# Attention with two exp engines: quarter-row pieces of the shifted exp tiles on GpSimd, placed beside VectorE's PSUM reads

## The chip, the cores and the metric

The kernel runs on one core of a Trainium2 chip. The metric is the device time of one execution in microseconds. I quote medians of a kernel's runs; a ratio is the mean time of one kernel's fast runs over the mean of the other's fast runs of the same rounds, so it is not quite the ratio of the medians. Among the fast runs the granted TensorE clock lay between 0.98 and 1.00, and the runs of one kernel spread by up to 0.8%, mostly with the lower clock at the slower end.

TensorE does matrix products into PSUM, ScalarE (ACT) does exp, VectorE (DVE) and GpSimd (POOL) do elementwise work; GpSimd does not read PSUM here. "Page" below is the printed summary of a profile.

## The reference, cut to what matters

```python
x = A_x                                   # 1 x 2048 x 512, bf16
xn = _layernorm(x)
q = heads(xn @ wq)                        # 32 heads of 16
k, v = xn @ wk, xn @ wv                   # one head of keys and values for all
p = softmax(q @ k.T * 16 ** -0.5)         # 32 x 2048 x 2048
s = merge(p @ v) @ wo
g = silu(silu(xn @ w1) @ w2)              # two-layer side branch
return x + s * g
```

The work is the 134 million exps. In tiles of 128 keys x 512 queries they are 2048 *score tiles*. Each is one matmul of the scores, one exp, and value matmuls.

## The kernel before

A planner in Python simulates the five engines with fixed durations and emits one static order for each, with semaphores. A score tile has two ways through:

- **ScalarE**: one exp over two or three PSUM banks at once, then one value matmul per tile.
- **VectorE**: a linear map of the score to the bits of a bf16 number, which is a coarse exp with a periodic error. Four copies of it with shifted bits, weighted in the value matmuls, average the error away. One tile costs one *eviction* (PSUM to SBUF, 128x512) and a quarter of four *shifts* (SBUF to SBUF, 128x2048, one for four tiles), and five value matmuls.

The eviction and the shift (everything else cut):

```python
# eviction, one per tile
bt.P[i] = pl.add(Task(DV, T_P, lambda v, b=b, i=i, bb=bt.b: v.tensor_scalar(
    db_sb[:, bb, i * NQ:(i + 1) * NQ], bank(b), 128.0 * LOG2E, 128.0 * SHIFT_BETA + 16256.0,
    op0=ALU.mult, op1=ALU.add), [("ps", b)], [("Db", bt.b, i)], ...))
# shift, four per batch of four tiles
pl.add(Task(DV, T_SH, lambda v, s=s, j=j, bb=bt.b: v.tensor_scalar(
    ds_sb[:, s, :], db_sb[:, bb, :], SHIFT[j], None, op0=ALU.add), ...))
```

How many tiles go to VectorE is decided while planning:

```python
def want_d(banks_left=True):
    # ... cut
    if dve_backlog() > DVE_LIMIT:        # 4000 ns
        return False
    return True
# in do_S, for each score phase of TensorE:
want = 2 if bl < TWO_LIMIT else 1        # 1500 ns of VectorE backlog
nd = min(cap, 4 - len(banks), len(need), want)
if nd < min(want, len(need)) and len(banks) == 3 and bl < LEND_LIMIT:
    nd, lend = nd + 1, True              # take a bank from ScalarE's three
```

The softmax here doesn't subtract the row's maximum and nothing guards it: scores larger than these inputs give would overflow.

## Time and profile before

770.08 us when first timed (768.81 to 770.92, 3 runs).

| from 100 to 730 us | TensorE | VectorE | ScalarE | GpSimd |
|---|---|---|---|---|
| busy, us of 630 | 590.4 | 617.3 | 630.0 | 0.0 |
| share | 94% | 98% | 100% | 0% |

The page: busy time of each engine, the chain of work that ended last, and three groups of instructions. A group's columns are line, engine, operation, tiles, forms and count, then busy us and mean ns of one, then the engine's idle us just before them.

```profile
span 768.8 us, 19950 instructions
PE 708.2 (92%) x8669; PEld 201.6 (26%) x8669; DVE 738.2 (96%) x1290; ACT 748.2 (97%) x773; POOL 20.0 (3%) x46
...
ACT 95%; DVE 1%; PE 1%; DMA 1%; issue 0%; SPq 0%; DVEq 0%
...
L1206 ACT ACTIVATE pa_sb<-ps 128x1024 bf16<-128x1024 f32 (+1 forms) x694 | 737.2, 1391 | 2.8 <-PE ps L697 2.7
L873 DVE TENSOR_SCALAR db_sb<-ps 128x512 uint16<-128x512 f32 x492 | 327.0, 685 | 11.2 <-PE ps L697 9.4
L907 DVE TENSOR_SCALAR ds_sb<-db_sb 128x2048 uint16<-128x2048 uint16 x492 | 321.7, 684 | 0.9
```

ScalarE's exp (L1206) waits 2.8 us in all, and the chain is ScalarE for 95%: the time is the amount of ScalarE's work. Evictions (L873) and shifts (L907) number 492 each, so 24% of the tiles go to VectorE, and VectorE is full. Three engines are full or nearly so, and one is empty.

Bars are longer than the distance between starts, because the start of one instruction overlaps the end of the last. The timeline of VectorE (start us, length us, merged runs of equal instructions) shows the distance:

```profile
312.30 0.68 DVE L907 TENSOR_SCALAR ds_sb<-db_sb 128x2048 uint16<-128x2048 uint16 x1
312.90 0.68 DVE L873 TENSOR_SCALAR db_sb<-ps 128x512 uint16<-128x512 f32 x1
313.50 0.68 DVE L907 TENSOR_SCALAR ds_sb<-db_sb 128x2048 uint16<-128x2048 uint16 x1
314.10 0.68 DVE L550 SCALAR_TENSOR_TENSOR tmp_sb<-t_sb,ps 128x512 bf16<-128x512 bf16 x1
```

Each costs 0.60 us of VectorE, not 0.68. A tile therefore takes 1.20 us of VectorE, half of it the shifts, and a quarter of a shift is 0.15 us.

### The profile page before, as it was taken

Reading aid. Unit: us, or ns where it says so; the run is one execution under the profiler, and the core shown is the slowest. Engines: PE = TensorE matmul, PEld = TensorE weight load, DVE = VectorE, ACT = ScalarE, POOL = GpSimd, SP = SyncE. Lnnn points to the kernel's source line nnn. Section 1 sums busy time; section 2 is a strip of 40 time slices with the busy share of each in tenths; the row PEclk is TensorE's granted clock in tenths of the full one; section 3 lists DMA queues with packets and bytes.
Section 4 is the critical chain, followed back from the end, with each engine's and each line's share of the span. In section 5 each row is a group of like instructions: output and inputs, shape, how many; then the busy total and the mean of one; then the engine's idle time right before and its main releaser. Section 6 shows DMA issues by size and latency. Waiting matters only on the chain.

```text
span 768.8 us, 19950 instructions
## 1 busy us (share of the span) xinstructions
PE 708.2 (92%) x8669; PEld 201.6 (26%) x8669; DVE 738.2 (96%) x1290; ACT 748.2 (97%) x773; POOL 20.0 (3%) x46
## 2 busy tenths in 40 slices
PE   8999999999989999999989999999998999999985
PEld 3322222222222222222222222222222222222222
DVE  7699999999999999999999999999999999999996
ACT  4999999999999999999999999999999999999995
POOL 5400000000000000000000000000000000000000
PEclk9999999999999999999999999999999999999999
DMA  9300000000000000000000010000000000000000
GB/s 312 88 1 2 2 2 1 2 2 2 2 1 15 29 15 2 1 2 2 2 1 2 15 29 15 2 2 2 3 1 2 15 15 29 2 2 2 1 2 28
DMA packets 11429, 12.57 MB, mean 16 GB/s; under 512 B 1808, under 2 KB 10768, under 8 KB 11344
## 3 DMA queue, kind: packets, MB, share of 16 engines
q1 hardware_dynamic: 10288, 11.28, 4.6%
q8 instruction: 69, 1.13, 0.6%
q10 hardware_dynamic: 1056, 0.03, 0.1%
q14 instruction: 16, 0.13, 0.1%
HBM read 8.95 MB, written 2.10 MB: 14 GB/s over the span
## 4 chain that ended last, share of the span: by engine, by line
ACT 95%; DVE 1%; PE 1%; DMA 1%; issue 0%; SPq 0%; DVEq 0%
ACT pa_sb L1206 91%; ACT t_sb L525 4%; ACT t_sb L548 1%; DMA ds_sb<-in_A_x_dram 1%; DVE stats_sb L359 1%; PE ps L697 0%; PE ps L440 0%; SPq L317 0%; PE ps L398 0%; PE ps L968 0%; PE ps L414 0%; DVE xnT_sb L425 0%; DVE f_sb L985 0%; DVE ob_sb L565 0%; DVE on_sb L996 0%
## 5 line engine op out<-in xcount | busy, mean ns | idle before, releaser
L1206 ACT ACTIVATE pa_sb<-ps 128x1024 bf16<-128x1024 f32 (+1 forms) x694 | 737.2, 1391 | 2.8 <-PE ps L697 2.7
L873 DVE TENSOR_SCALAR db_sb<-ps 128x512 uint16<-128x512 f32 x492 | 327.0, 685 | 11.2 <-PE ps L697 9.4
L907 DVE TENSOR_SCALAR ds_sb<-db_sb 128x2048 uint16<-128x2048 uint16 x492 | 321.7, 684 | 0.9
L697 PE MATMUL ps<-qt_sb,kt_sb 32*128 32x512 bf16 x2048 | 272.9, 384 | 47.7 <-ACT pa_sb L1206 35.9
L968 PE MATMUL ps<-ds_sb,v_sb 128*32 128x512 bf16 x1968 | 260.0, 383 | 0.8 <-DVE ds_sb L907 0.5
L968 PE MATMUL ps<-pa_sb,v_sb 128*32 128x512 bf16 x1556 | 257.5, 385 | 0.8 <-ACT pa_sb L1206 0.4
L697 PEld LDWEIGHTS ps<-qt_sb,kt_sb 32*128 32x128 bf16 x2048 | 69.9, 91 | 337.7 <-ACT pa_sb L1206 273.4
L968 PE MATMUL ps<-db_sb,v_sb 128*32 128x512 bf16 x492 | 133.7, 384 | 2.6 <-DVE f_sb L985 1.9
L968 PEld LDWEIGHTS ps<-ds_sb,v_sb 128*32 128x32 bf16 x1968 | 65.4, 95 | 56.5 <-issue 28.1
L968 PEld LDWEIGHTS ps<-pa_sb,v_sb 128*32 128x32 bf16 x1556 | 63.6, 94 | 52.5 <-issue 34.1
L398 PE MATMUL ps<-xnT_sb,w_sb 128*32 128x512 bf16 x896 | 76.6, 385 | 0.6 <-DVE u_sb L527 0.4
L398 PE MATMUL ps<-w_sb,u_sb 128*32 128x512 bf16 x896 | 75.8, 385 | 0.0
L525 ACT ACTIVATE t_sb<-ps 128x512 bf16<-128x512 f32 x56 | 48.8, 872 | 0.0
L527 DVE SCALAR_TENSOR_TENSOR u_sb<-t_sb,ps 128x512 bf16<-128x512 bf16 x56 | 38.1, 680 | 0.6 <-ACT t_sb L525 0.3
L968 PEld LDWEIGHTS ps<-db_sb,v_sb 128*32 128x32 bf16 x492 | 33.0, 94 | 20.4 <-issue 10.4
L398 PEld LDWEIGHTS ps<-xnT_sb,w_sb 128*32 128x32 bf16 x896 | 19.5, 94 | 33.1 <-issue 24.0
L985 DVE STREAM_TRANSPOSE f_sb<-ps 128x512 f32<-128x512 f32 x32 | 22.7, 710 | 5.0 <-PE ps L968 4.9
L398 PEld LDWEIGHTS ps<-w_sb,u_sb 128*32 128x32 bf16 x896 | 18.6, 94 | 31.0 <-issue 26.0
L398 PE MATMUL ps<-xnT_sb,wq_sb 128*32 128x512 bf16 x256 | 20.5, 383 | 0.0
L398 PE MATMUL ps<-wo_sb,on_sb 128*32 128x512 bf16 x256 | 19.9, 383 | 0.6 <-DVE on_sb L996 0.6
L548 ACT ACTIVATE t_sb<-ps 128x512 bf16<-128x512 f32 x16 | 13.8, 860 | 0.0
L989 DVE TENSOR_TENSOR otr_sb<-f_sb,rcp_sb 128x256 bf16<-128x256 f32 x32 | 13.3, 416 | 0.0
(46 smaller groups left out, 160.3 us busy)
## 6 DMA issues: line engine op xcount, KB each, us to landing
w_sb<-in_B_w_dram SPq DMA_DIRECT2D x2, 1792.0 KB, 13.2
xr_sb<-in_A_x_dram SPq DMA_DIRECT2D x16, 128.0 KB, 2.4
out_dram<-ob_sb SPq DMA_DIRECT2D x16, 128.0 KB, 1.7
ds_sb<-in_A_x_dram SPq DMA_DIRECT2D x3, 512.0 KB, 7.9
ds_sb<-in_A_x_dram SPq DMA_DIRECT2D x4, 128.0 KB, 2.6
wq_sb<-in_A_wq_dram SPq DMA_DIRECT2D x1, 512.0 KB, 5.9
wo_sb<-in_A_wo_dram SPq DMA_DIRECT2D x1, 512.0 KB, 14.5
kt_sb<-kt_sb SPq DMA_DIRECT2D x4, 64.0 KB, 2.3
```

The source lines that it names most:

```text
L359: ts_ = pl.add(Task(DV, 593.0, lambda v, t=t: v.bn_stats(stats_sb[:, t, :], x_tile(t)), [xkey(t)], [("st", t)], 1 + j, gate=(lambda: q_don ...
L398: last = h.matmul(bank(b)[32 * j:32 * (j + 1), 0:n], lhsT=lhs(j), rhs=rhs, start=start, stop=stop, tile_position=(0, 32 * j), skip_group_c ...
L525: t1 = Task(AC, 477.0, lambda a: a.activation(t_sb[:, k, :], bank(b), ACT.Tanh, scale=0.5), [("ps", b)], [("t", k)], 0)
L527: t2 = Task(DV, T_P, lambda v: v.scalar_tensor_tensor(out=u_sb[:, ft, :], in0=t_sb[:, k, :], scalar=1.0, in1=bank(b), op0=ALU.add, op1=ALU ...
L548: t1 = Task(AC, 477.0, lambda a: a.activation(t_sb[:, k, :], bank(b), ACT.Tanh, scale=0.25), [("ps", b)], [("t", k)], 0)
L697: return pe.matmul(bank(b), lhsT=kt_sb[32 * i:32 * i + 32, g % 2, kt * P:(kt + 1) * P], rhs=qt_sb[32 * i:32 * i + 32, (g // 2) % NQR, :], ...
L873: bt.P[i] = pl.add(Task(DV, T_P, lambda v, b=b, i=i, bb=bt.b: v.tensor_scalar(db_sb[:, bb, i * NQ:(i + 1) * NQ], bank(b), 128.0 * LOG2E, 1 ...
L907: pl.add(Task(DV, T_SH, lambda v, s=s, j=j, bb=bt.b: v.tensor_scalar(ds_sb[:, s, :], db_sb[:, bb, :], SHIFT[j], None, op0=ALU.add), [("Db" ...
L968: h = pe.matmul(bank(OB)[32 * i:32 * (i + 1), :], lhsT=lhs, rhs=rhs, start=s0, stop=s1, tile_position=(0, 32 * i), skip_group_check=True)
L985: t1 = pl.add(Task(DV, T_TR, lambda v: v.transpose(f_sb[:, k, :], bank(OB)), [("ps", OB)], [("F", k)], 1, [norm.get(("m", g - 2))]))
L989: t3 = pl.add(Task(DV, 332.0, lambda v: v.tensor_tensor(o3[:, :, val:val + DH], f3[:, :, val:val + DH], rcp_sb[:, k, :].unsqueeze(2).to_br ...
L1206: op = pl.place(AC, 0.8333 * NQ * n + T_AF, lambda a: a.activation(pa_sb[:, s, 0:n * NQ], ps[:, b0 * 512:(b0 + n) * 512], ACT.Exp), [("ps" ...
```

## The change

Intent: give part of the shifts to idle GpSimd. The Trainium skill, "SBUF — State Buffer", section "Who interferes with whom", says that VectorE shares one pair of SBUF ports with GpSimd, that a VectorE tensor_scalar from SBUF to SBUF can run in a mode that takes this pair for the whole instruction, that the second comer "fully blocks", and that an instruction with at most one SBUF input outside those modes does not contend. So a shift on GpSimd is cut in quarters of 128x512, each about as long as one eviction; a quarter is planned only while VectorE's last planned instruction is a PSUM read (or another one-port instruction) with at least half a piece left to run; and the planner holds back either engine's two-port instruction while the other's runs. Each shift is offered to both engines, and whichever takes it first removes it from the other.

```diff
+T_PC, PC_FIT = 600.0, 0.5
@@ Planner
+    def locked(self, eng, ports):
+        if ports != 2 or eng not in self.lock:
+            return 0.0
+        return self.lock[PO if eng == DV else DV]
@@ place
-            t0 = max(self.clk[eng], self.ready(eng, reads, writes))
+            t0 = max(self.clk[eng], self.ready(eng, reads, writes), self.locked(eng, ports))
+        if eng in self.lock and ports == 2:
+            self.lock[eng] = op.end
@@ make_shifts: split(bt, s, j) replaces the single VectorE task
+            sh.whole = pl.add(Task(DV, T_SH, ..., on_place=placed_dv, ports=2))
+            for i in range(4):
+                tk = Task(PO, T_PC, lambda g, i=i: g.tensor_scalar(
+                    ds_sb[:, s, i * NQ:(i + 1) * NQ], db_sb[:, bt.b, i * NQ:(i + 1) * NQ], 1.0, SHIFT[j],
+                    op0=ALU.mult, op1=ALU.add), ...
+                    gate=lambda i=i: (sh.owner is None if i == 0 else sh.owner == PO and sh.chunks[i - 1].op is not None)
+                    and beside_psum_read(), ports=2)
+                tk.after = before_po
+                sh.chunks.append(pl.add(tk))
+        def beside_psum_read():
+            last = pl.order[DV][-1]
+            return last.ports == 1 and last.end - max(pl.clk[PO], pl.lock[DV], pl.lock[PO]) >= PC_FIT * T_PC
# cut: ports=2 on three other VectorE tasks, bookkeeping, tuple priorities, the case of an empty order, and
# before_po, which makes a piece wait for the last VectorE instruction planned to be done when it starts
```

More of the change, by code (lines that the diff above doesn't have):

```diff
@@ L47, with __init__ @@
 class Op:
-    __slots__ = ("eng", "emit", "deps", "idx", "inc", "val", "t0", "end", "vis", "dma", "know", "sem", "waits")
+    __slots__ = ("eng", "emit", "deps", "ports", "idx", "inc", "val", "t0", "end", "vis", "dma", "know", "sem", "waits")
 class Task:
-    __slots__ = ("eng", "dur", "emit", "reads", "writes", "prio", "preds", "op", "on_place", "dma", "gate")
-    def __init__(self, eng, dur, emit, reads=(), writes=(), prio=5, preds=(), on_place=None, dma=0, gate=None):
+    __slots__ = ("eng", "dur", "emit", "reads", "writes", "prio", "preds", "op", "on_place", "dma", "gate", "ports", "after")
+    def __init__(self, eng, dur, emit, reads=(), writes=(), prio=5, preds=(), on_place=None, dma=0, gate=None, ports=1):
+        self.ports, self.after = ports, None
         self.eng, self.dur, self.emit = eng, dur, emit
@@ L79, in __init__ @@
         self.dma_t = 0.0
+        self.lock = {DV: 0.0, PO: 0.0}
     def vis(self, op, eng):
@@ L107, in ready, with place @@
         return r
-    def place(self, eng, dur, emit, reads, writes, dma=0, t0=None):
+    def place(self, eng, dur, emit, reads, writes, dma=0, t0=None, ports=1, after=None):
         op = Op()
-        op.eng, op.emit, op.inc, op.val, op.know, op.sem = eng, emit, False, 0, None, None
+        op.eng, op.emit, op.inc, op.val, op.know, op.sem, op.ports = eng, emit, False, 0, None, None, ports
         deps = self.deps(eng, reads, writes)
+        if after is not None:
+            deps.append(after)
         seen = set()
@@ L147, in avail @@
             return None
-        return self.ready(task.eng, task.reads, task.writes)
+        return max(self.ready(task.eng, task.reads, task.writes), self.locked(task.eng, task.ports))
     def place_task(self, task):
         self.tasks[task.eng].remove(task)
-        task.op = self.place(task.eng, task.dur, task.emit, task.reads, task.writes, task.dma)
+        task.op = self.place(task.eng, task.dur, task.emit, task.reads, task.writes, task.dma,
+                             ports=task.ports, after=task.after() if task.after else None)
         if task.on_place:
@@ L162, in best @@
             if r <= t + 25.0:
-                key = (task.prio() if callable(task.prio) else task.prio, k)
+                p = task.prio() if callable(task.prio) else task.prio
+                key = (p if isinstance(p, tuple) else (p,), k)
                 if now is None or key < now[0]:
@@ L377, in bass_recurrent_scan__grouped_kv_mqa__dense_activation_silu__prompt_kernel @@
                     op0=ALU.subtract, op1=ALU.mult),
-                    [xkey(t), ("rs", pr), ("mv", t)], [("xn", t % 4)], 1 + t // 4, [t2],
+                    [xkey(t), ("rs", pr), ("mv", t)], [("xn", t % 4)], 1 + t // 4, [t2], ports=2,
                     gate=lambda t=t: t < 4 or t - 4 in t_done))
@@ L565, in final @@
             t2 = Task(DV, 333.0, lambda v: v.tensor_tensor(ob_sb[:, tt % 4, :], fin_sb[:, k, :], xr_sb[:, tt % 4, :], ALU.add),
-                      [("fin", k), ("xr", tt % 4)], [("ob", tt % 4)], 1, [t1, xr_task[tt], out_task.get(tt - 4)])
+                      [("fin", k), ("xr", tt % 4)], [("ob", tt % 4)], 1, [t1, xr_task[tt], out_task.get(tt - 4)], ports=2)
             t3 = Task(SP, 60.0, lambda e: e.dma_start(of.rearrange("(t p) d -> p t d", p=P)[:, tt, :], ob_sb[:, tt % 4, :]),
@@ L899, in make_shifts @@
                     j = bt.nsh
-                    def placed(pop, j=j, s=s, bt=bt):
-                        release(bt)
-                        for i in range(4):
-                            kt = bt.slots[i]
-                            pvq[bt.g][i].append((pop, v_lhs(j + 1, bt.g, kt), ds_sb[:, s, i * NQ:(i + 1) * NQ].bitcast(BF16),
-                                                 ds_keys(s) + v_reads(j + 1, kt), ("s", s)))
-                    pl.add(Task(DV, T_SH, lambda v, s=s, j=j, bb=bt.b: v.tensor_scalar(
-                        ds_sb[:, s, :], db_sb[:, bb, :], SHIFT[j], None, op0=ALU.add),
-                        [("Db", bt.b, i) for i in range(4)], ds_keys(s),
-                                lambda g=bt.g: URGENT if g == st["gO"] and nleft[g] <= CLOSING else 6, list(bt.P.values()), on_place=placed))
+                    split(bt, s, j)
@@ new lines, in bass_recurrent_scan__grouped_kv_mqa__dense_activation_silu__prompt_kernel, with split, queue, placed_dv @@
+        class Shift:
+            pass
+        shifts = []
+        def split(bt, s, j):
+            sh = Shift()
+            sh.owner = None
+            def queue(pop, i):
+                kt = bt.slots[i]
+                pvq[bt.g][i].append((pop, v_lhs(j + 1, bt.g, kt), ds_sb[:, s, i * NQ:(i + 1) * NQ].bitcast(BF16),
+                                     [("Ds", s, i)] + v_reads(j + 1, kt), ("s", s)))
+            def placed_dv(pop):
+                sh.owner = DV
+                for tk in sh.chunks:
+                    pl.tasks[PO].remove(tk)
+                release(bt)
+                for i in range(4):
+                    queue(pop, i)
+            def placed_po(pop, i):
+                if sh.owner is None:
+                    sh.owner = PO
+                    pl.tasks[DV].remove(sh.whole)
+                queue(pop, i)
+                if i == 3:
+                    release(bt)
+            sh.whole = pl.add(Task(DV, T_SH, lambda v: v.tensor_scalar(
+                ds_sb[:, s, :], db_sb[:, bt.b, :], SHIFT[j], None, op0=ALU.add),
+                [("Db", bt.b, i) for i in range(4)], ds_keys(s),
+                lambda: URGENT if bt.g == st["gO"] and nleft[bt.g] <= CLOSING else 6,
+                list(bt.P.values()), on_place=placed_dv, ports=2))
+            sh.chunks = []
+            for i in range(4):
+                tk = Task(PO, T_PC, lambda g, i=i: g.tensor_scalar(
+                    ds_sb[:, s, i * NQ:(i + 1) * NQ], db_sb[:, bt.b, i * NQ:(i + 1) * NQ], 1.0, SHIFT[j],
+                    op0=ALU.mult, op1=ALU.add),
+                    [("Db", bt.b, i)], [("Ds", s, i)], (0 if i else 1, -len(shifts), i), list(bt.P.values()),
+                    on_place=lambda pop, i=i: placed_po(pop, i),
+                    gate=lambda i=i: (sh.owner is None if i == 0 else sh.owner == PO and sh.chunks[i - 1].op is not None)
+                    and beside_psum_read(), ports=2)
+                tk.after = before_po
+                sh.chunks.append(pl.add(tk))
+            shifts.append(sh)
@@ L912, in bass_recurrent_scan__grouped_kv_mqa__dense_activation_silu__prompt_kernel, with before_po @@
+        def beside_psum_read():
+            if not pl.order[DV]:
+                return False
+            last = pl.order[DV][-1]
+            return last.ports == 1 and last.end - max(pl.clk[PO], pl.lock[DV], pl.lock[PO]) >= PC_FIT * T_PC
+        def before_po():
+            t0 = max(pl.clk[PO], pl.lock[DV])
+            for op in reversed(pl.order[DV]):
+                if pl.vis(op, PO) <= t0 + 20.0:
+                    return op
+            return None
         x_free = [False]
@@ L991, in make_norm @@
                 rcp_sb[:, k, :].unsqueeze(2).to_broadcast([P, NQ // 32, DH]), ALU.mult),
-                [("F", k), ("rcp", k)], [("otr", oi % 2, e)], 3, [t2, t2_task.get(oi - 2)]))
+                [("F", k), ("rcp", k)], [("otr", oi % 2, e)], 3, [t2, t2_task.get(oi - 2)], ports=2))
             norm[("m", g)] = t3
```

## The prediction

> **What bounds the kernel now.** By the chain of waits, 95% of the 768.8 us span is ScalarE, 91% of it the exp of PSUM scores (694 instructions). By the groups, ScalarE waited 2.8 us for those scores: once begun it never stops, and the time is its work. The only way to shorten it is to give scores to VectorE, which computes exp by a linear map into bf16 bits (492 PSUM evictions of 128x512, 685 ns each) and four shifted copies per batch of four tiles (492 SBUF copies of 128x2048, 684 ns). The windows from 100 to 750 us show ScalarE at 100%, VectorE at 98%, TensorE at 94%: VectorE sets how many scores go its way (492 of 2048), ScalarE pays for the rest.
>
> **What the change moves.** Back to back, both VectorE kinds start 0.60 us apart in the timeline, so a score costs VectorE 0.60 + 0.60 = 1.20 us. A shift may now go to GpSimd as four 128x512 pieces, each placed beside a VectorE instruction that reads PSUM. By the Trainium skill, "SBUF — State Buffer", section "Who interferes with whom", a 16-bit SBUF-to-SBUF tensor_scalar holds the port pair that VectorE shares with GpSimd for the whole instruction and the second comer blocks; a PSUM eviction does not use it. No run here shows it yet. GpSimd is idle after 60 us.
>
> Nothing is removed in total. A piece saves VectorE 0.15 us. One piece per eviction, plus some beside the roughly 150 other PSUM reads, gives 500 to 650 pieces: 25 to 30% of the shifts (f).
>
> **Sum.** ScalarE: T = 70 + (2048 - d) x 0.449 us, which at d = 492 gives 769 (start, tail and 72 tanh in the 70). VectorE: T = 178 + d x (1.202 - 0.601 f), fitted the same way. With f = 0.25 to 0.30, d = 541 to 552 and T = 747 to 742 us. All saved ScalarE time is on the critical path. TensorE gets four more value matmuls per moved score, about 50 to 60 rounds of 0.216 us (12 us), less about 20 score phases of 0.43 us; over a shorter span its share rises from 94 to about 96.5%: tight, not quite binding.
>
> **Losses.** The planner assumes 600 ns per piece. From this trace: a GpSimd COPY of 256 bf16 occupies 0.34 us to the next start, and memsets grow by about 0.83 ns per element, so 512 elements need an estimated 0.56 us; but its tensor_scalar of only 64 elements took 0.42 us, from which 0.8 us would follow. Anything over 0.60 blocks the next VectorE shift by the excess, and each late piece can hold up TensorE's fixed order. I take 8 to 10 us back: 753 us.
>
> **What the profile would show.** Right: 500 to 650 GpSimd pieces of 600 to 720 ns; 370 to 400 VectorE shifts left; 530 to 555 evictions; ScalarE exp falling by 20 to 28 us, still at 99% and waiting under 10 us; eviction duration unchanged at 685 ns; a few VectorE shifts longer than 700 ns. Wrong: shift mean above 800 ns (lock collisions), or evictions lengthened (the PSUM read contends too), or ScalarE waiting tens of us for scores (TensorE or late pieces bind).
>
> **What would make it wrong.** Pieces of 750 ns or more: the lock returns the saving, and time stays at 760 to 775. TensorE saturating during the two-layer job rounds. Shifts spread over four pieces holding their output buffers longer, so batches start later. On the other side, a lock that hardly costs and well-packed pieces would reach 742.
>
> Predicted: 753 us, 8 in 10 between 741 and 770; faster by over 2% (under 754.7) 0.53, within 2% 0.43, slower 0.04.

## The result, and the profile after

750.3 us (749.11 to 752.35, 4 runs) against 770.05 us; ratio 0.9745, 95% interval 0.9725 to 0.9765.

| | before | after |
|---|---|---|
| evictions (tiles on VectorE) | 492 | 540 |
| shifts on VectorE | 492 | 380 |
| pieces on GpSimd | 0 | 640 (= 160 shifts) |
| exp instructions (three-bank / two-bank) | 168 / 526 | 106 / 595 |
| VectorE busy, 100 to 730 us | 617.3 | 606.7 |
| TensorE busy, 100 to 730 us | 590.4 | 607.9 |

The page of the kernel after, the same parts (in the changed source L1272 is the exp, L887 the eviction, L947 the shift, L954 the piece):

```profile
span 748.0 us, 21011 instructions
PE 709.1 (95%) x8809; PEld 200.9 (27%) x8809; DVE 703.7 (94%) x1226; ACT 727.6 (97%) x780; POOL 498.1 (67%) x686
...
ACT 95%; DVE 1%; PE 1%; DMA 1%; POOL 0%; issue 0%; SPq 0%; ACTq 0%; DVEq 0%
...
L1272 ACT ACTIVATE pa_sb<-ps 128x1024 bf16<-128x1024 f32 (+1 forms) x701 | 715.5, 1333 | 2.8 <-PE ps L711 2.7
L954 POOL TENSOR_SCALAR ds_sb<-db_sb 128x512 uint16<-128x512 uint16 x640 | 478.2, 758 | 215.1 <-DVE ds_sb L947 101.1
L887 DVE TENSOR_SCALAR db_sb<-ps 128x512 uint16<-128x512 f32 x540 | 357.2, 682 | 23.3 <-PE ps L711 21.2
...
L947 DVE TENSOR_SCALAR ds_sb<-db_sb 128x2048 uint16<-128x2048 uint16 x380 | 249.6, 682 | 1.5
```

The chain is still ScalarE for 95%, and the exp still waits 2.8 us. Its busy time fell by 737.2 - 715.5 = 21.7 us, the span by 20.8. That is the whole result: 48 tiles left ScalarE, and nothing was added to its waits. Evictions and shifts each still take 682 ns: neither was made slower by GpSimd.

The mean of 758 ns of the pieces hides two main kinds. Counted from the trace, 394 of the 640 last under 640 ns (mean 616); the 227 whose bar starts while a shift is running last 1007 ns on average. The other 19 last 720 to 768 ns, and each starts while VectorE runs a tensor_tensor with both inputs in SBUF (into `otr_sb` or `ob_sb`), which the change also marks `ports=2`. The profiler's spans on GpSimd are rough; from start to start the closest pieces are 0.581 us apart. The timeline shows one that started in a shift (VectorE and GpSimd lines alone):

```profile
309.21 1.29 DVE L947 TENSOR_SCALAR ds_sb<-db_sb 128x2048 uint16<-128x2048 uint16 x2
309.98 0.99 POOL L954 TENSOR_SCALAR ds_sb<-db_sb 128x512 uint16<-128x512 uint16 x1 [1.43 <-DVE ds_sb L947]
310.42 0.68 DVE L887 TENSOR_SCALAR db_sb<-ps 128x512 uint16<-128x512 f32 x1
311.02 0.68 DVE L947 TENSOR_SCALAR ds_sb<-db_sb 128x2048 uint16<-128x2048 uint16 x1
```

The piece starts at 309.98 in the middle of the second shift, which ends at 310.50, and ends at 310.97. It lasted 0.38 us longer than a free one, and it was done before the next shift at 311.02: its own work lay beside the eviction of 310.42. The planner issues pieces so that the port itself is the last gate. Waiting costs GpSimd time of which it has plenty.

### The profile page after: what moved, and what is told of

It reads as the page before. It is cut to its first block, busy times and chain, and to the rows that moved or that the text cites. A ratio compares the mean times of both kernels' runs of the same rounds, so it can differ in the third digit from the quotient of the medians.

```text
span 748.0 us, 21011 instructions
## 1 busy us (share of the span) xinstructions
PE 709.1 (95%) x8809; PEld 200.9 (27%) x8809; DVE 703.7 (94%) x1226; ACT 727.6 (97%) x780; POOL 498.1 (67%) x686
## 4 chain that ended last, share of the span: by engine, by line
ACT 95%; DVE 1%; PE 1%; DMA 1%; POOL 0%; issue 0%; SPq 0%; ACTq 0%; DVEq 0%
ACT pa_sb L1272 91%; ACT t_sb L539 4%; ACT t_sb L562 1%; DMA ds_sb<-in_A_x_dram 1%; DVE stats_sb L373 0%; PE ps L412 0%; POOL v_sb L496 0%; SPq L331 0%; PE ps L428 0%; DVE xn_sb L389 0%; PE ps L1034 0%; PE ps L711 0%; ACTq L277 0%; DVE ob_sb L579 0%; POOL rstd_sb L385 0%
## 5 line engine op out<-in xcount | busy, mean ns | idle before, releaser
L1272 ACT ACTIVATE pa_sb<-ps 128x1024 bf16<-128x1024 f32 (+1 forms) x701 | 715.5, 1333 | 2.8 <-PE ps L711 2.7
L954 POOL TENSOR_SCALAR ds_sb<-db_sb 128x512 uint16<-128x512 uint16 x640 | 478.2, 758 | 215.1 <-DVE ds_sb L947 101.1
L887 DVE TENSOR_SCALAR db_sb<-ps 128x512 uint16<-128x512 f32 x540 | 357.2, 682 | 23.3 <-PE ps L711 21.2
L1034 PE MATMUL ps<-ds_sb,v_sb 128*32 128x512 bf16 x2160 | 286.7, 382 | 0.2
L1034 PE MATMUL ps<-pa_sb,v_sb 128*32 128x512 bf16 x1508 | 267.2, 385 | 1.1 <-ACT pa_sb L1272 0.7
L947 DVE TENSOR_SCALAR ds_sb<-db_sb 128x2048 uint16<-128x2048 uint16 x380 | 249.6, 682 | 1.5
L1034 PE MATMUL ps<-db_sb,v_sb 128*32 128x512 bf16 x540 | 145.0, 384 | 1.6 <-DVE f_sb L1051 1.6
L1034 PEld LDWEIGHTS ps<-ds_sb,v_sb 128*32 128x32 bf16 x2160 | 71.8, 95 | 54.7 <-issue 32.4
L539 ACT ACTIVATE t_sb<-ps 128x512 bf16<-128x512 f32 x56 | 48.1, 858 | 0.0
L496 POOL TENSOR_SCALAR v_sb<-v_sb 128x64 bf16<-128x64 f32 x24 | 8.9, 373 | 9.4 <-DVE v_sb L492 6.1
```

The lines of the kernel that those rows point to most:

```text
L496: v_task[c, j] = pl.add(Task(PO, 150.0, lambda g, j=j: g.tensor_scalar(v_sb[:, j, 4 * c:4 * c + 4, DH:2 * DH], v32_sb[:, 4 * c:4 * c + 4, ...
L539: t1 = Task(AC, 477.0, lambda a: a.activation(t_sb[:, k, :], bank(b), ACT.Tanh, scale=0.5), [("ps", b)], [("t", k)], 0)
L947: sh.whole = pl.add(Task(DV, T_SH, lambda v: v.tensor_scalar(ds_sb[:, s, :], db_sb[:, bt.b, :], SHIFT[j], None, op0=ALU.add), [("Db", bt.b ...
L954: tk = Task(PO, T_PC, lambda g, i=i: g.tensor_scalar(ds_sb[:, s, i * NQ:(i + 1) * NQ], db_sb[:, bt.b, i * NQ:(i + 1) * NQ], 1.0, SHIFT[j], ...
L1034: h = pe.matmul(bank(OB)[32 * i:32 * (i + 1), :], lhsT=lhs, rhs=rhs, start=s0, stop=s1, tile_position=(0, 32 * i), skip_group_check=True)
L1272: op = pl.place(AC, 0.8333 * NQ * n + T_AF, lambda a: a.activation(pa_sb[:, s, 0:n * NQ], ps[:, b0 * 512:(b0 + n) * 512], ACT.Exp), [("ps" ...
```

## The experiments

Where an edit below leaves the piece loop in use, one line was needed besides, because with other offers the planner can end with a started shift whose last pieces find no PSUM read any more. It is in every variant of the changed kernel below except `blind_quarter`; alone it leaves the counts of the plan at 540, 380 and 640:

```diff
-                    and beside_psum_read(), ports=2)
+                    and (beside_psum_read() or i > 0 and st["assigned"] == NG * SLOTS), ports=2)
```

### 1 and 2. Does the gain go with the number of pieces?

```diff
-            for i in range(4):
+            for i in range(4 if len(shifts) % 8 == 7 else 0):   # dose_eighth
+            for i in range(4 if j == 4 else 0):                 # dose_quarter
                 tk = Task(PO, T_PC, ...
```

> Only every eighth shift is offered to GpSimd (248 pieces instead of 640, 508 evictions in the program; everything else as in the changed kernel). Theory 1 (each piece frees 0.15 us of VectorE, which is spent on more evictions and so fewer exps): the gain of 19.75 us goes with the pieces, 248/640 of it, so about 762 us (760 to 764), exp waiting under 5 us. Rival 1 (the gain is that VectorE gets slack and no longer sits at 98%, so a few pieces suffice): most of the gain, 752 to 757 us. Rival 2 (the order of the plan, not the pieces, brings the gain): no relation to the count.

Measured: 763.46 us (762.55 to 763.98), ratio 0.9923 (0.9908 to 0.9937). The page shows 248 pieces and 508 evictions.

> One shift of the four of each batch is offered to GpSimd (520 pieces, 532 evictions in the program). Theory 1: 520/640 of 19.75 us, so about 754 us (752 to 756). This is the partner of blind_quarter: the same offers, pieces beside PSUM reads.

Measured: 753.04 us (752.39 to 754.59), ratio 0.9791 (0.9775 to 0.9808), with 520 pieces and 532 evictions.

Against 769.01 us in these rounds the gains are 5.6 us for 248 pieces, 16.0 for 520, and 19.75 for 640 in the first comparison: 0.022, 0.031 and 0.031 us per piece. The small dose returned somewhat less than its share, the opposite of "a few pieces suffice"; part of that is in the plan, which handed VectorE 16 more tiles for 248 pieces, 40 for 520 and 48 for 640. The gain goes with the work taken off VectorE. Nor can the new planner code alone explain it: with no piece offered it emits, instruction for instruction, the program of the kernel before (492 evictions, 492 shifts, 694 exps).

### 3. Does it matter where the pieces lie?

The same offers as in `dose_quarter`, but with no lock in the plan and no gate:

```diff
-            for i in range(4):
+            for i in range(4 if j == 4 else 0):
...
-                    and beside_psum_read(), ports=2)
+                    , ports=1)
```

> The same offers as dose_quarter (532 pieces, 532 evictions in the program), but the planner knows no lock and places pieces anywhere, also during and before VectorE shifts. Theory of the lock (a piece and a VectorE shift exclude each other for the whole instruction): VectorE loses up to 0.58 us where a piece runs as a shift comes up; with an average loss of 0.1 to 0.2 us on some 300 to 500 pieces that is 30 to 100 us of VectorE time, partly hidden; the static orders of TensorE and ScalarE then wait too: 765 to 800 us, shift starts delayed (start-to-start above 0.70 us on average after a piece), ScalarE waiting tens of us. Rival (the lock does not matter in practice, or GpSimd alone pays for it): 752 to 757 us like dose_quarter.

Measured: 798.42 us (796.51 to 799.44), ratio 1.0378 (1.0354 to 1.0403): 45 us slower than its partner with the same 532 evictions (and 532 pieces where the partner has 520), and slower than the kernel before. Lock and gate were taken out together, so their shares are not told apart.

Groups by form of `dose_quarter` and then of `blind_quarter`:

```profile
L887 DVE TENSOR_SCALAR db_sb<-ps 128x512 uint16<-128x512 f32 x532 | 352.1, 682 | 17.2 <-PE ps L711 14.5
L947 DVE TENSOR_SCALAR ds_sb<-db_sb 128x2048 uint16<-128x2048 uint16 x402 | 264.6, 681 | 1.2
...
L1272 ACT ACTIVATE pa_sb<-ps 128x1024 bf16<-128x1024 f32 x603 | 608.3, 1278 | 0.7 <-PE ps L711 0.7
```

```profile
L887 DVE TENSOR_SCALAR db_sb<-ps 128x512 uint16<-128x512 f32 x532 | 345.6, 675 | 7.6 <-PE ps L711 7.0
L947 DVE TENSOR_SCALAR ds_sb<-db_sb 128x2048 uint16<-128x2048 uint16 x399 | 321.7, 828 | 1.4
...
L1272 ACT ACTIVATE pa_sb<-ps 128x1024 bf16<-128x1024 f32 x600 | 583.0, 1054 | 25.6 <-PE ps L711 23.2
```

The shift rose from 681 to 828 ns, 399 x 0.147 = 59 us of VectorE in all. Counted from the trace, the 200 shifts that start while a piece's bar is running last 983 ns on average, the other 199 last 672. ScalarE began to wait: 25.6 us before its two-bank exps alone, instead of 0.7. Evictions did not lengthen. A blocked shift in the timeline of `blind_quarter`:

```profile
299.12 1.62 POOL L954 TENSOR_SCALAR ds_sb<-db_sb 128x512 uint16<-128x512 uint16 x2
299.61 0.67 DVE L887 TENSOR_SCALAR db_sb<-ps 128x512 uint16<-128x512 f32 x1
300.20 1.08 DVE L947 TENSOR_SCALAR ds_sb<-db_sb 128x2048 uint16<-128x2048 uint16 x1
301.21 1.27 DVE L887 TENSOR_SCALAR db_sb<-ps 128x512 uint16<-128x512 f32 x2
```

The eviction beside the first piece keeps its 0.67 us. The shift that begins at 300.20, while the second piece runs until 300.74, lasts 1.08 us. The skill's rule ("SBUF — State Buffer", "Who interferes with whom") agrees in both directions: the second comer waits, and a PSUM read is not touched.

### 4. Why quarters?

Pieces of 128x1024, two per shift, planned at 1.025 us:

```diff
-T_PC, PC_FIT = 600.0, 0.5
+T_PC, PC_FIT = 1025.0, 0.5
-            for i in range(4):
+            for i in range(2):
# cut: slices, keys and queueing of two tiles per piece
```

> Each piece is half a tile row (128x1024, two per shift), planned at 1.025 us, an estimate from 0.58 us for 512 elements and a slope of 0.83 to 0.87 ns per element; gate of one half kept. A piece then outlasts one PSUM eviction of 0.60 us, so the following shift is held unless another PSUM read comes. Theory of the lock: the gain shrinks: 349 shifts left on VectorE but up to 0.4 us lost after a piece, 754 to 760 us. Rival (piece size does not matter, fixed cost per piece dominates and larger is better): 745 to 750 us.

Measured: 757.27 us (756.64 to 758.04), ratio 0.9844 (0.9829 to 0.9858), 7 us slower than quarters. One line of `halves` (count, then shortest, median and longest bar in ns; the count at the end of the line is of a sample):

```profile
L955 POOL TENSOR_SCALAR ds_sb<-db_sb x350: 1039/1417/1549, 37.7 to 731.6; 128x1024 uint16<-128x1024 uint16 x175
```

A free piece is 1.04 us, longer than the 0.60 us of one eviction. Counted from the trace, 36 of the 349 shifts last over 720 ns (3 of 380 with quarters), and VectorE's idle time before evictions is 37.5 us instead of 23.3. The halves move more work than the quarters (350 pieces are 175 shifts, against 160), yet fewer tiles go to VectorE (524). That the planner, which knows the lock, avoids the collision and pays with idle time is my reading; it was not separated, and the profile names TensorE as the releaser of 33.7 of the 37.5 us. Closest starts of pieces are 1.009 us apart here and 0.581 with quarters: 0.428 us for 512 more elements, 0.84 ns each, and about 0.15 us fixed.

### 5 to 8. Did TensorE, at 97%, eat part of the gain?

In the kernel after, TensorE is busy for 607.9 of 630 us and VectorE waits longer for scores, so TensorE was the natural suspect. Two reliefs test it, alone and together. Both compute something else than the reference on purpose (they happened to stay within the tolerance of the output comparison, which says nothing for them).

```diff
# tensor relief, in the kernel before and in the changed one: only 2 of the 14 contraction rounds of each
# z tile (a tile of the product with w2 in the side branch) are kept
-  job("z", ..., [(rnd(ft), ["w2", ("u", ft)], MM) for ft in range(NFT)], consume,
+  job("z", ..., [(rnd(ft), ["w2", ("u", ft)], MM) for ft in range(0, NFT, NFT - 1)], consume,
# vector relief: half the shift on VectorE; value matmuls of such a shift read its first half twice
-  sh.whole = pl.add(Task(DV, T_SH, ... ds_sb[:, s, :], db_sb[:, bt.b, :], SHIFT[j], ...
+  sh.whole = pl.add(Task(DV, 335.0, ... ds_sb[:, s, 0:2 * NQ], db_sb[:, bt.b, 0:2 * NQ], SHIFT[j], ...
```

> The kernel before with 12 of the 14 contraction rounds of each of the 16 z tiles left out (wrong result on purpose): 192 rounds x 0.216 = 41 us less TensorE work. 492 evictions as before. Both theories: 767 to 771 us, for TensorE waits 36 us for ScalarE there.

Measured: 768.98 us (767.26 to 771.7), ratio 0.999 (0.9963 to 1.0017).

> The changed kernel with the same 41 us of TensorE work left out (wrong result on purpose); 540 evictions, as in the changed kernel. Theory A (TensorE at 97% busy only looks full: ScalarE waits 2.8 us for it, so it is not what holds the time): 748 to 751 us. Theory B (TensorE became the bottleneck and ate part of the gain): clearly faster, 735 to 745 us.

Measured: 750.38 us (748.23 to 753.99), ratio 0.975 (0.9715 to 0.9785), against 0.9745 without the relief. Two lines of its page:

```profile
PE 676.4 (91%) x8129; PEld 194.6 (26%) x8129; DVE 702.6 (94%) x1226; ACT 725.8 (97%) x749; POOL 508.8 (68%) x686
...
L887 DVE TENSOR_SCALAR db_sb<-ps 128x512 uint16<-128x512 f32 x540 | 356.8, 682 | 15.1 <-PE ps L711 12.6
```

TensorE's busy time in the profile fell from 709.1 to 676.4 us (33 us, less than the 41 planned) and the time did not move. TensorE does not hold the time of the kernel after. The planner, which knew of the lighter load, still gave VectorE 540 tiles. VectorE's wait before evictions fell from 23.3 to 15.1 us, but its idle time in all hardly did: span less busy time is 43.9 us here and 44.3 in the kernel after.

> The changed kernel with VectorE's own shifts cut to half their length (128x1024, 0.335 us instead of 0.60; wrong result on purpose): about 100 us less VectorE work, so the planner sends 600 scores its way instead of 540. If VectorE alone limits: 60 x 0.45 = 27 us less, about 723 us. If the next limit, TensorE, lies close behind (four more value matmuls per moved score): no gain, 745 to 770 us, and ScalarE begins to wait for scores, tens of us instead of 2.8.

Measured: 758.88 us (758.32 to 760.43), ratio 0.986 (0.9839 to 0.9881): slower than the kernel after, although VectorE's work fell and 600 tiles went its way. Exps of `vector_relief_after`:

```profile
L1273 ACT ACTIVATE pa_sb<-ps 128x1024 bf16<-128x1024 f32 x649 | 624.8, 1231 | 18.0 <-PE ps L711 17.9
L1273 ACT ACTIVATE pa_sb<-ps 128x1536 bf16<-128x1536 f32 x48 | 79.2, 1650 | 1.7 <-PE ps L711 1.6
```

ScalarE has less to do (704.4 us busy in all) but the exps now wait 19.7 us, nearly all of it for TensorE's scores: ScalarE is no longer always busy.

> Both reliefs at once (wrong result on purpose): 616 evictions. If TensorE is the limit right behind VectorE: 725 to 740 us, so that the two together give what neither gives alone. If something else holds the time (the PSUM banks, the buffers, GpSimd): like the worse of the two single reliefs, 745 or more.

Measured: 728.99 us (728.26 to 729.89), ratio 0.9468 (0.9452 to 0.9483). The exps wait 4.6 us, with 616 tiles on VectorE.

So the kernel after sits close to a corner. Taking work off TensorE alone brings nothing and off VectorE alone costs 9 us, but both together bring 21. Much cheaper shifts would run into TensorE; at 540 tiles it is not yet reached.

### 9 to 11. What was left: VectorE waiting for scores

The idle time of VectorE before evictions doubled, from 11.2 to 23.3 us, with TensorE as releaser. TensorE's load is part of that wait (8 us of it went in experiment 6) but does not set the number of tiles, which stayed at 540 there. The suspect that remained is the planner's rule for handing tiles out: one tile per score phase (a turn of TensorE's score matmuls) unless the backlog of VectorE is under 1.5 us. With shifts gone to GpSimd, that queue may run dry more often. Six constants were set anew by a search over the plan (its planned end, not a time of the chip):

```diff
-DVE_LIMIT = 4000.0
-MARGIN, MARGIN_END = 16, 28
-LEND_LIMIT = 3000.0
-TWO_LIMIT = 1500.0
-CLOSING, URGENT = 3, 1.5
-NPA, PRESS = 9, 4
+DVE_LIMIT = 4500.0
+MARGIN, MARGIN_END = 18, 28
+LEND_LIMIT = 3250.0
+TWO_LIMIT = 3000.0
+CLOSING, URGENT = 3, 3.0
+NPA, PRESS = 9, 5
```

> The changed kernel with six constants of the planner set anew, chosen for a plan that keeps VectorE supplied with scores (564 evictions, 388 shifts, 704 pieces in the program instead of 540, 380, 640). If VectorE's 23 us of waiting for scores is the slack left in the changed kernel, 24 more scores leave ScalarE: 24 x 0.45 = 11 us off, so 739 us (736 to 743), VectorE waiting under 10 us before evictions. Rival (TensorE at 97% cannot take it, its lateness returns the gain): 747 to 752 us, ScalarE waiting over 10 us.

Measured: 739.78 us (739.57 to 741.47), ratio 0.962 (0.9603 to 0.9637), correct. VectorE's groups of `tuned_after`:

```profile
L887 DVE TENSOR_SCALAR db_sb<-ps 128x512 uint16<-128x512 f32 x564 | 372.1, 683 | 6.5 <-PE ps L711 4.2
L947 DVE TENSOR_SCALAR ds_sb<-db_sb 128x2048 uint16<-128x2048 uint16 x388 | 258.3, 681 | 1.8 <-PE ps L1034 1.6
```

The idle time before evictions is 6.5 us, and 24 more tiles left ScalarE. The new plan also moves 16 more shifts to GpSimd (704 pieces), 16 x 0.60 = 9.6 us of VectorE, so the gain is not that of the shorter waits alone. TensorE took it (602.1 of 620 us from 100 to 720 us), and the exps wait 1.7 us. This version beats both kernels.

> Control: the same six constants in the kernel before (500 evictions instead of 492). If the constants help by themselves: 8 x 0.45 = 3.6 us, about 766 us (764 to 768). So most of the gain of tuned_after would need the pieces. Rival (the constants were simply bad, and do the same for both): 758 to 762 us.

Measured: 769.18 us (766.27 to 771.04), ratio 0.9997 (0.9976 to 1.0018). I expected 766: a miss. The 8 tiles did leave ScalarE (500 evictions in the page, 684 exps instead of 694), and the profiled run had a span of 764.2 us against 768.8, but the timed runs show no gain beyond their spread. They had lower granted clocks (0.985 to 0.996) than the kernel before in the same rounds (0.991 to 0.999): its two runs at 0.996 took 766.3 and 766.4 us, where the kernel before took 768.4 to 769.3 us at 0.997 or more, so the medians may hide a gain of 2 to 3 us. Either way these constants bring nothing like 10 us without the pieces. A search made for the kernel before was not tried.

```diff
-TWO_LIMIT = 1500.0
-NPA, PRESS = 9, 4
+TWO_LIMIT = 3000.0
+NPA, PRESS = 9, 5
```

> Only two of the six: two scores at a time go to VectorE while its backlog is under 3.0 us (was 1.5), and partial value rounds are forced from five busy exp buffers (was four); 556 evictions: 16 x 0.45 = 7 us off, 743 us (741 to 746).

Measured: 743.37 us (742.62 to 745.23), ratio 0.9665 (0.9647 to 0.9684). By the ratios (0.9665 against 0.962 and 0.9745, times 769 us) two of the six constants bring about 6 of the 10 us. The two were changed together, so their shares are not told apart, nor is each of the six.

### 12. Is the second operation of the piece a cost?

```diff
-  ds_sb[...], db_sb[...], 1.0, SHIFT[j], op0=ALU.mult, op1=ALU.add)
+  ds_sb[...], db_sb[...], SHIFT[j], None, op0=ALU.add)
```

> The piece as one operation (add) instead of two (multiply by 1.0, then add); the program's order is the same. If GpSimd's time per element is set by reading and writing: pieces that start free stay at 0.61 us, 749 to 752 us. If the second operation costs: they get shorter, the time hardly moves (the plan still assumes 0.60). If the one-operation form takes a slower path: pieces above 0.7 us, and time above 755 us by the lock.

Measured, in one look: 1139.63 us, correct. The order of the program is unchanged. A single run has no known state, and its granted clock of 0.822 is lower than that of the other runs, but the effect is far beyond that. One line of the pieces and the chain of `one_op`:

```profile
L954 POOL TENSOR_SCALAR ds_sb<-db_sb x640: 1482/1491/2394, 37.1 to 1118.0; 128x512 uint16<-128x512 uint16 x160
```

```profile
POOL 77%; PE 10%; DVE 8%; issue 3%; ACT 1%; DMA 1%; SPq 0%; POOLq 0%; ACTq 0%; DVEq 0%
```

Of the three outcomes listed the third came, far beyond its size: the plainer instruction took 1.48 us instead of 0.61. GpSimd became the chain (640 pieces x 1.455 us, the closest from start to start, = 931 us), and TensorE waited for late pieces in its fixed order (234.7 us before its value matmuls, by the profile). The multiplication by 1.0 is not decoration; it is what lets the piece fit beside an eviction. Why the one-operation form is slow stays open; only this add on uint16 was run.

## Why the prediction was right or wrong

The time was foretold as 753 (741 to 770) and measured as 750.3, over 2% faster. Point by point:

- **What bounds it, and what the tile is worth: right.** T = 70 + (2048 - d) x 0.449 gives 747.1 us for d = 540, and the profiled span is 748.0; for d = 564 it gives 736.3, and `tuned_after` shows 737.8. ScalarE waited 2.8 us before and after.
- **How many pieces: right.** 640 (500 to 650 foretold), 380 shifts left (370 to 400), 540 evictions (530 to 555), exp busy time down 21.7 us (20 to 28). The share of shifts moved is 160/540 = 0.30.
- **Length of a piece: half right.** The copy-based estimate of 0.56 us was close to the 0.581 us measured between starts. The other one, 0.8 us from the small tensor_scalar in the trace of before, came from a one-operation instruction; experiment 12 shows that form to be slow, so it was a poor guide to the two-operation piece (that small multiply itself was not tested). The foretold bar of 600 to 720 ns holds for 395 of the 640; the others mostly carry the wait for the port in their bar, which I had not thought of as the normal case. So the warning "pieces of 750 ns or more: the lock returns the saving" was met by the mean of 758 ns and still did not come true: what made the mean long was pieces waiting for shifts, not pieces that held shifts up.
- **The loss of "8 to 10 us": the size was about right, the cause was wrong, so that part of the hit is luck.** I put it down to pieces that outlast evictions and block shifts, and to late pieces. In the kernel after, only 3 of 380 shifts are over 720 ns, and the exps wait no longer than before. The sum had given 742 us at f = 0.30. It was fitted to the span, and the span was 748.0 us in the run that was timed at 749.77, so about 6 us are missing, not 8. By VectorE's sum, 540 tiles at f = 0.296 take 731 us, and the span was 17 us longer. Of these, 12.1 us are longer waits for scores (23.3 us instead of 11.2 before evictions); the rest is not explained. By the slopes of the two sums, 17 us of VectorE are worth 17 x 0.449 / (1.024 + 0.449) = 5 us of time, an estimate that covers most of the 6. `tuned_after` got about 10 us back (0.962 against 0.9745 of 769 us) with the same kind of pieces and the same lock, but also with 16 more shifts moved, so it does not isolate the waiting.
- **"Shift mean above 800 ns (lock collisions)" as the sign of failure: right as a sign.** It is what `blind_quarter` shows, 828 ns at 798 us. The change avoids it by placement.
- **TensorE "tight, not quite binding": right.** Foretold at about 96.5%; 607.9/630 = 96.5% measured, and a relief that took 33 us off its busy time brought nothing. One step beyond, at 600 tiles, it binds.

## What to carry to other kernels

When two engines share a port that one instruction holds as a whole, cut the weaker engine's share into pieces no longer than the other engine's port-free instructions, and put the lock into the plan: from the same offers, 520 pieces gained 16 us with it and 532 cost 29 us without it. Once work has left a full engine, look at what now feeds that engine; half as much gain again lay in six constants of the planner that hands out the work, set for the old balance. Read the two populations inside a mean before believing it, and measure the exact form of an instruction before trusting a neighbour's cost.

## What the Trainium skill lacked or had wrong

- "GPSIMD Engine Reference", section "Elementwise — side-by-side cycle accounting": it gives a port-bound 1.03 cycles per element for bodies of at most two operations. The two-operation piece agrees (0.84 ns per element from experiment 4, by estimate 1.00 cycle at the 1.2 GHz of that page's section "Specifications"). The page does not say that a tensor_scalar with one operation can be far slower than one with two: 1482 ns against 611 ns for 128x512 uint16, shortest bars.
- The same section gives a ratio of 1.96 to VectorE for an fp32 tensor_tensor add, and has none for a 16-bit shift from SBUF to SBUF: here a quarter row takes 0.581 us on GpSimd, and a quarter of a whole shift is 0.15 us on VectorE, 3.9 times.
- "SBUF — State Buffer", section "Who interferes with whom": confirmed, with numbers. Beside pieces, evictions from PSUM stay at 682 ns (685 without); a piece that comes second lasts 1007 ns on average instead of 616; in the blind plan shifts last 828 ns instead of 681. The waiting time lies inside the bar of the blocked instruction, so this profile shows it as a longer instruction and not as idle time; that section does not say where to look for it.
- The page "SBUF — State Buffer", section "A bandwidth-pool intuition that's wrong (but worth ruling out)", puts the end of the block about 115 ns after VectorE's instruction, for a DMA whose descriptors GpSimd has to write; it gives no figure for a GpSimd instruction. Here a blocked piece ends 0.476 us (median) after the bar of the shift, sooner than the 0.611 us of the shortest free piece, so part of its start seems to overlap the wait; how much was not separated.
